# Rotated queries and keys of two chunks in one tile, for the first batch of a linear-attention and MoE kernel

## The chip, the cores and the metric

One core of a Trainium2 chip runs the whole program. The metric is the device time of one execution in microseconds (us). The engines are PE (matrix products), DVE (VectorE), ACT (ScalarE), POOL (GpSimd) and SP (the queue from which most transfers are issued).

## The reference, cut to what matters

Attention is a recurrence with a complex decay for every key feature; two MoE-like layers follow, the second behind a Fourier transform.

```python
# q, k, v, a_re, a_im: 4 batches, 8 heads, 768 steps, 48 features
scale = min(|a|, 0.999) / (|a| + 1e-6);  a = a * scale
for t in range(768):
    S_re, S_im = a.re*S_re - a.im*S_im + outer(k[t], v[t]),  a.re*S_im + a.im*S_re
    y[t] = q[t] @ S_re
u  = y + (U, V mixing of y over the steps)
x1 = u + relu(u @ w_ch1) @ w_ch2
u  = x1 + real(fft2(x1));  un = layernorm(u)
out = u + relu(un @ w_ch1') @ w_ch2'
```

## The kernel before

The recurrence is done in 6 chunks of 128 steps for each batch. Within a chunk the decay is split into a magnitude (folded into q and k) and an angle; q and k, multiplied by the cosine and sine of the summed angle, stand in 96 rows per head (48 features, real and imaginary). A chunk then needs the products of keys and queries (scores), a mask, the product with v, and a state that is carried to the next chunk. Chunks come in pairs m of two; `PAIRS` holds three pairs for each batch, and a tile that is loaded or made elementwise covers both chunks of a pair (index j).

`decays(m)` makes the magnitudes, `turns(m)` the angles. For the first pair (m = 0) `parts(m)` lets `turns` treat the two chunks one after the other, for all others at once. At its end `turns` writes for each chunk the tile QK: two copies of the end magnitudes (L426, the last two of 258 columns) and keys and queries times cosine and sine (L430, two VectorE instructions a chunk, for 2 x 3 rows of 128 steps each). Partition 8x + h of QK holds feature x of 16 and head h. The 96-row layout QT, in which features stand in partitions, is made by six transfers (L437): for each of z (cosine, sine) and i (three groups of 16 features) the 128 partitions of QK go to 16 partitions of QT, eight heads side by side, 258 floats (1032 bytes) from each partition. ScalarE makes the scaled keys from QK (L433).

`products(m, j)` consumes a chunk: scores on PE from QT (L462), masking on VectorE (`pm`, L467), transposed keys `kp` (L476) split into `k` (L481, L482), the state factor `fe` on POOL from QT (L537), the outputs `y` and the state sum `g` (L490), the state S (L564 on POOL, L575 on VectorE, L573 on ScalarE for the first).

`first_attention` runs batch 0 with nothing beside it but the first weights. Weights of the MoE layer come in 24 halves: a load into `stw` (L117, with buffers shared with `k` of batch 0, five in all), ACT L110, DVE L110, L132 and L133, a rounding copy on ACT (L147), and the low part on POOL (L148). `decays(3)`, for batch 1, is also written there. Then the MoE of batch 0 runs on PE (`hp` and `acc`, L93 to L95), with the attention of batch 1 beside it, and so on. A list scheduler sets the order on each engine from the program's priorities; at run time each engine runs its list in order, and an instruction that waits holds those behind it. At most eight transfers of the SP queue are under way: the ninth waits for the first.

Pools: `att` lives through all attention. `early` opens ahead of batch 0's attention and closes with it; `halves` opens then, in the memory that `early` leaves. Before the change QK and QT have two buffers in `att`, and chunks 2 and 5 of batch 0 have one in `early`:

```python
where = dict(pl=early[0], bufs=1) if b == 0 and c % 3 == 2 else dict(bufs=2)
QK = at(f"QK{b}_{c}", "QK", shape=(128, 2, 3, 258), **where)
QT = at(f"QT{b}_{c}", "QT", shape=(96, 8, 258), **where)
```

So chunk 3 takes chunk 0's buffers, chunk 4 chunk 1's, and chunk 5 chunk 2's.

Of the kernel before, what the change touches and what calls it, by code (L numbers as in the profile page):

```python
# [43 lines left out]
def mixer_kernel(ctx, tc, a_in, qk_in, v_in, u_in, v4_in, w_in, cc_in, ss_in, cb_in, sb_in, id_in, mask_in, rows_in, out):  # L44
    nc = tc.nc
# [13 lines left out]
    def bank(name, pool=None):  # L59
        pool = pool or pms  # L60
        return pool.tile([128, 512], F32, tag={id(pms): "ms", id(pacc): "acc", id(phid): "hid"}[id(pool)], name=name)
# [21 lines left out]
    def use(name):  # L83
        if table[0] != name:
            ordered(lambda: A.preload_act_table_set(name))
            table[0] = name

    def tabled(*args, **kw):
        ordered(lambda: A.activation(*args, **kw))  # L89
# [8 lines left out]
    early = [None]  # L98
# [121 lines left out]
    def attention_pool():  # L220
        pl = attp[0]

        def at(nm, tag=None, bufs=4, shape=(128, 3, 2, 128), dt=F32, pl=pl):
            return pl.tile(list(shape), dt, tag=tag or "t", name=nm, bufs=bufs)

        return at
# [32 lines left out]
    def row(x, i, js):  # L259
        return x[:, i, js].rearrange("p j t -> p (j t)")  # L260

    def flat(x):
        return x.rearrange("p i j t -> p (i j t)")

    def parts(m):

        return [slice(0, 1), slice(1, 2)] if m == 0 else [slice(0, 2)]
# [111 lines left out]
    def turns(m):  # L379

        b, cc = PAIRS[m]
        at = attention_pool()
        T_, Th, qf, kf, ends, turn, scaled = ew[m]
        use(TRIG)
        jj = parts(m)
        for js in jj:
            tabled(T_[:, :, js], T_[:, :, js], AF.Arctan, scale=1.0 / RE_MID)
        yield
        QKs = {}
        for js in jj:  # L390
            cy = carry.get(b)
            t, th = T_[:, :, js], Th[:, :, js]
            if len(jj) == 1:
                if cy is not None:
                    V.tensor_tensor(T_[:, :, 0, 0], T_[:, :, 0, 0], cy[:, :3], ALU.add)
                V.tensor_tensor_scan(out=flat(Th), data0=going, data1=flat(T_), initial=0.0, op0=ALU.mult, op1=ALU.add)
            else:
                for i in range(3):
                    V.tensor_tensor_scan(
                        out=row(Th, i, js),  # L400
                        data0=one.to_broadcast([128, 128]),
                        data1=row(T_, i, js),
                        initial=0.0 if cy is None else cy[:, i : i + 1],
                        op0=ALU.mult,
                        op1=ALU.add,
                    )
            if b == 0:
                V.tensor_scalar(t, th, 1.0 / (2 * PI), MAGIC, ALU.mult, ALU.add)
            else:
                A.activation(t, th, AF.Copy, bias=MAGIC, scale=1.0 / (2 * PI))  # L410
            V.scalar_tensor_tensor(out=th, in0=t.bitcast(I16)[:, :, :, 0::2], scalar=-2 * PI, in1=th, op0=ALU.mult, op1=ALU.add)
            c = cc[js.stop - 1]
            if c != NC - 1:
                carry[b] = at(f"cy{b}_{c}", "cy", 2, (128, 4))
                V.tensor_copy(carry[b][:, :3], Th[:, :, js.stop - 1, 127])
            tabled(t, th, AF.Sin, scale=1.0 - 2.0**-22)
            A.activation(th, th, AF.Abs)
            tabled(th, th, AF.Sin, bias=halfpi, scale=-1.0)
            yield
            if len(jj) == 1:  # L420
                yield
            for j in range(js.start, js.stop):
                c = cc[j]
                where = dict(pl=early[0], bufs=1) if b == 0 and c % 3 == 2 else dict(bufs=2)
                QK = at(f"QK{b}_{c}", "QK", shape=(128, 2, 3, 258), **where)
                V.tensor_copy(QK[:, :, :, 256:258], ends[:, :, j : j + 1].unsqueeze(1).to_broadcast([128, 2, 3, 2]))  # L426
                QT = at(f"QT{b}_{c}", "QT", shape=(96, 8, 258), **where)
                w = turn[:, :, :, j]
                for to, x in ((slice(128, 256), kf), (slice(0, 128), qf)):
                    V.tensor_tensor(QK[:, :, :, to], x[:, :, j].unsqueeze(1).to_broadcast([128, 2, 3, 128]), w, ALU.mult)  # L430
                if c != NC - 1:
                    for i in range(3):
                        A.activation(scaled[:, :, i, j], QK[:, :, i, 128:256], AF.Copy, scale=ends[:, i, j : j + 1])  # L433
                for z in range(2):
                    for i in range(3):
                        p0 = z * 48 + i * 16
                        nc.sync.dma_start(QT[p0 : p0 + 16], QK[:, z, i, :])  # L437
                qkt[b, c] = QT, scaled[:, :, :, j]
                yield

    def products(m, j):

        b, cc = PAIRS[m]
        c = cc[j]
        n = f"{b}_{c}"
        last = c == NC - 1
        plain = b <= 1
        at = attention_pool()

        def t3(nm, bufs, shape, dt=F32):  # L450
            return at(f"{nm}{n}", nm, bufs, shape, dt, attp[1] if dt == F16 else attp[0])

        QT, scaled = qkt[b, c]
        vin = inp["v", b, c]
        sc, pm, kp = [], [], []
        pool = pacc if b == 0 else pms

        def scores(hf):
            ps = bank(f"sc{n}_{hf}").rearrange("p (h t) -> p h t", h=4)
            for h in range(4):  # L460
                q = QT[:, hf * 4 + h]
                T.matmul(ps[:, h, :], q[:, 128:256], q[:, :128], start=True, stop=True)  # L462
            sc.append(ps)

        def masked(hf):
            pm.append(room[:, hf] if b == 0 else at(f"pm{n}_{hf}", "pm", 2, (128, 4, 128)))
            V.tensor_tensor(pm[hf], sc[hf], mask.unsqueeze(1).to_broadcast([128, 4, 128]), ALU.mult)  # L467
            if not plain:
                hs = slice(hf * 4, hf * 4 + 4)
                A.copy(ph[:, hs], pm[hf])  # L470
                V.tensor_tensor(plo[:, hs], pm[hf], ph[:, hs], ALU.subtract)
# [27 lines left out]
        if b == 0:  # L499
            if len(rooms) < 4:  # L500
                rooms.append(wpl.tile([128, 3, 4, 128], F32, tag="w", name=f"pm{n}"))
            room = rooms[c % 4]
# [12 lines left out]
        yield  # L515
        scores(1)
        masked(0)
        if not plain and c > 0:
            qh, ql = t3("qh", 1, (96, 8, 128), F16), t3("ql", 1, (96, 8, 128), F16)
            A.copy(qh, QT[:, :, :128])  # L520
            V.tensor_tensor(ql, QT[:, :, :128], qh, ALU.subtract)
        yield
        masked(1)
        if not last:
            if b == 0:
# [166 lines left out]
    def elementwise(m):  # L692
        return padded(chain(decays(m), turns(m)), 16) if m < len(PAIRS) else iter(())
# [4 lines left out]
    def attention(b):  # L698
        m = 3 * b
        yield from padded(urgent(turns(m), -300) if b == 1 else turns(m), 9)  # L700
        ahead = chain(elementwise(m + 1), elementwise(m + 2), decays(m + 3) if b + 1 < B else ())
        yield from zipped(chain(padded(both(m), 16 + LAG), padded(both(m + 1), 16), both(m + 2)), ahead)
# [5 lines left out]

    def first_attention(w1):
        run(zipped(decays(0), late(1, decays(1)), late(2, decays(2))), turns(0))  # L710
        with tc.high_priority(-800):
            load_uv()
# [233 lines left out]
    attp = [apool.enter_context(tc.tile_pool(name="att", bufs=2)), None]  # L946
# [20 lines left out]
    warm, wide = bank("warm", phid)[:, :256], ident  # L967
# [261 lines left out]
```

## Time and profile before

| | us |
|---|---|
| median of three runs (lowest, highest) | 1006.13 (1005.81, 1008.61) |
| the profiled execution, its own time | 1010.51 |
| span of the profiled execution | 1008.7 |
| PE busy in the span | 867.8 (86%) |
| DVE busy | 643.1 (64%) |
| ACT busy | 466.6 (46%) |
| POOL busy | 224.9 (22%) |
| share of the chain that ended last that is DMA QT<-QK | 8% |

The span runs from the first to the last instruction of one execution; the time of an execution holds it and what lies around it. Busy shares are means over stages with different limits, so a stage has to be read from its own windows. The chain that ended last is followed back from the last instruction, at each step to what released it. Idle time in a timeline row stands in square brackets, with what ended it; an engine that is not the bound of its stage loses nothing by it.

### The profile page before, as it was taken

The numbers are of one execution on the slowest core, as the hardware profiler recorded it, in microseconds if no ns is written. First come the engines' busy times: TensorE is split into PE (matmuls) and PEld (weight loads), VectorE is DVE, ScalarE is ACT, GpSimd is POOL, SyncE is SP. The second block draws the span as 40 slices with busy tenths as digits, with TensorE's granted clock in tenths as the row PEclk, the third lists the DMA queues.
The fourth block names the chain that finished last, engine by engine and source line by source line (L and its number), as shares of the span: only waits on it lengthen the run. The fifth ranks groups of instructions, "written<-read, shape, count | busy, mean of one in ns | idle before, by whom it ended". The sixth has DMA issues, their size and how long they took to land.

```text
span 1008.7 us, 16225 instructions
## 1 busy us (share of the span) xinstructions
PE 867.8 (86%) x6350; PEld 821.9 (81%) x6350; DVE 643.1 (64%) x1110; ACT 466.6 (46%) x891; POOL 224.9 (22%) x227
## 2 busy tenths in 40 slices
PE   0056858798898898989999999799999999999997
PEld 0045747787887898878999999689999999999997
DVE  7967696767567796787873539986535635453121
ACT  8556557565775877768742223453112212211111
POOL 4312362302012010120205216532401312010000
PEclk9998677988998999989999999999999999999999
DMA  9049546463653627346055114341210101000000
GB/s 355 1 64 155 146 136 131 102 102 104 103 95 79 104 79 119 81 91 105 9 88 204 40 32 134 109 149 33 65 46 17 58 23 47 1 25 24 1 24 27
DMA packets 47093, 83.39 MB, mean 83 GB/s; under 512 B 5600, under 2 KB 36064, under 8 KB 47008
## 3 DMA queue, kind: packets, MB, share of 16 engines
q1 hardware_dynamic: 45152, 75.96, 33.3%
q0 software_dynamic: 1856, 6.31, 1.9%
q8 instruction: 52, 0.85, 0.4%
q14 instruction: 33, 0.27, 0.1%
HBM read 53.79 MB, written 9.44 MB: 63 GB/s over the span
## 4 chain that ended last, share of the span: by engine, by line
PE 46%; DVE 24%; DMA 13%; ACT 8%; issue 4%; SPq 4%; POOL 1%; another core or an unknown queue 0%; ACTq 0%; DVEq 0%; POOLq 0%
DMA QT<-QK 8%; PE acc L95 6%; PE hp L93 6%; PE hp L95 6%; PE hp L94 6%; PE acc L93 6%; PE acc L94 6%; DMA stw<-in_w_dram 5%; SPq L437 4%; PE sc L462 3%; DVE ls L354 2%; DVE QK L430 2%; DVE wxw L133 1%; ACT ls L89 1%; DVE wxw L132 1%
## 5 line engine op out<-in xcount | busy, mean ns | idle before, releaser
L193 DVE SCALAR_TENSOR_TENSOR hl<-hp,hh 128x384 fp32r<-128x384 f32 x192 | 105.6, 552 | 201.0 <-ACT hh L191 193.3
L191 ACT ACTIVATE hh<-hp 128x384 fp32r<-128x384 f32 x192 | 93.4, 488 | 273.9 <-PE hp L95 253.7
L93 PE MATMUL acc<-w,hh 128*128 128x384 f32 x576 | 204.0, 354 | 5.9 <-ACT hh L191 4.8
L94 PE MATMUL acc<-w,hh 128*128 128x384 f32 x576 | 198.8, 345 | 0.0
L95 PE MATMUL acc<-w,hl 128*128 128x384 f32 x576 | 164.7, 351 | 17.6 <-DVE hl L193 17.4
L95 PEld LDWEIGHTS acc<-w,hl 128*128 128x128 f32 x576 | 106.4, 194 | 23.6 <-DVE hl L193 23.1
L93 PEld LDWEIGHTS acc<-w,hh 128*128 128x128 f32 x576 | 111.8, 194 | 10.5 <-ACT hh L191 8.6
L94 PEld LDWEIGHTS acc<-w,hh 128*128 128x128 f32 x576 | 112.3, 195 | 0.2
L93 PE MATMUL hp<-u,w 128*128 128x384 f32 x288 | 101.2, 355 | 11.4 <-ACT u L639 11.4
L94 PE MATMUL hp<-u,w 128*128 128x384 f32 x288 | 103.2, 358 | 0.0
L95 PE MATMUL hp<-u,w 128*128 128x384 f32 x288 | 101.8, 353 | 0.0
L94 PE MATMUL hp<-n,w 128*128 128x384 f32 x288 | 96.5, 335 | 1.4 <-DVE n L917 1.2
L95 PE MATMUL hp<-n,w 128*128 128x384 f32 x288 | 96.5, 335 | 0.0
L93 PE MATMUL hp<-n,w 128*128 128x384 f32 x288 | 96.3, 335 | 0.0
L462 PE MATMUL sc<-QT 96*128 96x128 f32 x384 | 59.8, 311 | 28.7 <-DMA QT<-QK 23.5
L462 PEld LDWEIGHTS sc<-QT 96*128 96x128 f32 x384 | 55.1, 219 | 32.9 <-issue 30.3
L148 POOL TENSOR_TENSOR w<-wxw,w 128x384 fp32r<-128x384 f32 x48 | 57.5, 1202 | 75.1 <-ACT w L147 72.9
L93 PEld LDWEIGHTS hp<-u,w 128*128 128x128 f32 x288 | 57.7, 202 | 12.8 <-ACT u L639 12.8
L94 PEld LDWEIGHTS hp<-u,w 128*128 128x128 f32 x288 | 57.5, 200 | 1.1 <-DVE u L640 0.8
L95 PEld LDWEIGHTS hp<-u,w 128*128 128x128 f32 x288 | 57.3, 199 | 0.4
L94 PEld LDWEIGHTS hp<-n,w 128*128 128x128 f32 x288 | 54.1, 188 | 2.0 <-DVE n L917 2.0
L537 POOL TENSOR_SCALAR fe<-QT 96x8 f32<-96x8 f32 x20 | 6.5, 325 | 216.4 <-DMA QT<-QK 211.4
(285 smaller groups left out, 1747.3 us busy)
## 6 DMA issues: line engine op xcount, KB each, us to landing
QT<-QK SPq DMA_DIRECT2D x144, 129.0 KB
stw<-in_w_dram SPq DMA_DIRECT2D x48, 384.0 KB
ain<-in_a_dram SPq DMA_DIRECT2D x12, 768.0 KB
qkin<-in_qk_dram SPq DMA_DIRECT2D x12, 768.0 KB
x1d<-x SPq DMA_DIRECT2D x24, 192.0 KB
vin<-in_v_dram SPq DMA_DIRECT2D x18, 192.0 KB
lo<-x1d SPq DMA_DIRECT2D x12, 192.0 KB
out_dram<-lo SPq DMA_DIRECT2D x12, 192.0 KB
```

The lines of the kernel that those rows point to most:

```text
L89: ordered(lambda: A.activation(*args, **kw))
L93: T.matmul(o, ah, bh, start=start, stop=False, skip_group_check=skip)
L94: T.matmul(o, ah, bl, start=False, stop=False, skip_group_check=skip)
L95: T.matmul(o, al, bh, start=False, stop=stop, skip_group_check=skip)
L132: V.scalar_tensor_tensor(out=xi, in0=xi, scalar=3, in1=low, op0=ALU.logical_shift_left, op1=ALU.bitwise_or)
L148: G.tensor_tensor(w[:, 1, zs], x, f32(w[:, 0, zs]), ALU.subtract)
L191: A.activation(hh, hp, AF.Relu)
L193: V.scalar_tensor_tensor(out=hl, in0=hp, scalar=0.0, in1=f32(hh), op0=ALU.max, op1=ALU.subtract)
L354: V.tensor_tensor_scan(out=flat(s1), data0=starts, data1=flat(s1), initial=1.0, op0=ALU.max, op1=ALU.mult)
L430: V.tensor_tensor(QK[:, :, :, to], x[:, :, j].unsqueeze(1).to_broadcast([128, 2, 3, 128]), w, ALU.mult)
L437: nc.sync.dma_start(QT[p0 : p0 + 16], QK[:, z, i, :])
L462: T.matmul(ps[:, h, :], q[:, 128:256], q[:, :128], start=True, stop=True)
```

## The change

For batch 0 one tile QK holds both chunks of a pair, with the two chunks side by side for each z and i, and one tile QT likewise. It has one buffer for QK and two for QT, both in `early`. For the first pair the six transfers are still issued for each chunk (1032 bytes from each partition); for the second and third pair they are issued once, when the second chunk's products are done, and carry both chunks (2064 bytes from each partition). For the other batches a tile holds one chunk as before, in two buffers, but in `halves`. The masked scores `pm` of the later batches move to `halves` as well.

```diff
@@ turns
-        QKs = {}
+        wide = b == 0
+        n_j = 2 if wide else 1
+        pl = early[0] if b == 0 else attp[1]
         for js in jj:
...
             for j in range(js.start, js.stop):
                 c = cc[j]
-                where = dict(pl=early[0], bufs=1) if b == 0 and c % 3 == 2 else dict(bufs=2)
-                QK = at(f"QK{b}_{c}", "QK", shape=(128, 2, 3, 258), **where)
+                if j == 0 or not wide:
+                    QKs = at(f"QK{b}_{c}", "QK", 1 if wide else 2, (128, 2, 3, n_j, 258), pl=pl)
+                    QTs = at(f"QT{b}_{c}", "QT", 2 if b == 0 or not wide else 1, (96, 8, n_j, 258), pl=pl)
+                jw = j if wide else 0
+                QK, QT = QKs[:, :, :, jw], QTs[:, :, jw]
                 V.tensor_copy(QK[:, :, :, 256:258], ends[:, :, j : j + 1].unsqueeze(1).to_broadcast([128, 2, 3, 2]))
-                QT = at(f"QT{b}_{c}", "QT", shape=(96, 8, 258), **where)
                 w = turn[:, :, :, j]
                 for to, x in ((slice(128, 256), kf), (slice(0, 128), qf)):
                     V.tensor_tensor(QK[:, :, :, to], x[:, :, j].unsqueeze(1).to_broadcast([128, 2, 3, 128]), w, ALU.mult)
+                if not wide or m == 0 or j == 1:
+                    at_j = slice(jw, jw + 1) if m == 0 else slice(0, n_j)
+                    for z in range(2):
+                        for i in range(3):
+                            p0 = z * 48 + i * 16
+                            nc.sync.dma_start(
+                                QTs[p0 : p0 + 16, :, at_j].rearrange("p h j t -> p h (j t)"),
+                                QKs[:, z, i, at_j].rearrange("p j t -> p (j t)"),
+                            )
                 if c != NC - 1:
...
-                for z in range(2):
-                    for i in range(3):
-                        p0 = z * 48 + i * 16
-                        nc.sync.dma_start(QT[p0 : p0 + 16], QK[:, z, i, :])
                 qkt[b, c] = QT, scaled[:, :, :, j]
@@ products, masked
-            pm.append(room[:, hf] if b == 0 else at(f"pm{n}_{hf}", "pm", 2, (128, 4, 128)))
+            pm.append(room[:, hf] if b == 0 else at(f"pm{n}_{hf}", "pm", 2, (128, 4, 128), pl=attp[1]))
```

The scheduler makes a new order of it on all engines, up to about 300 us of the profile; behind that the order is the same on each. In the names below the first digit is the batch and the next the chunk (or, for `stw` and `w`, the layer, f and half); the last number only tells buffers apart.

SP's queue, from the transfers of chunk 0 on, before:

```order
L437 DMA QT0_0_225<-QK0_0_223 16x8x258 x6
L437 DMA QT0_1_249<-QK0_1_247 16x8x258 x6
L437 DMA QT0_2_331<-QK0_2_329 16x8x258 x6
L437 DMA QT0_3_354<-QK0_3_352 16x8x258 x6
L117 DMA stw0_0_0_594<-in_w_dram 128x768
L117 DMA stw0_0_1_596<-in_w_dram 128x768
L117 DMA stw0_1_0_606<-in_w_dram 128x768
L437 DMA QT0_4_415<-QK0_4_413 16x8x258 x6
L437 DMA QT0_5_457<-QK0_5_455 16x8x258 x6
L117 DMA stw0_1_1_711<-in_w_dram 128x768
```

and now:

```order
L440 DMA QT0_0_224<-QK0_0_223 16x8x258 x12
L117 DMA stw0_0_0_576<-in_w_dram 128x768
L440 DMA QT0_2_328<-QK0_2_327 16x8x516 x6
L117 DMA stw0_0_1_578<-in_w_dram 128x768
L117 DMA stw0_1_0_588<-in_w_dram 128x768
L440 DMA QT0_4_404<-QK0_4_403 16x8x516 x6
L117 DMA stw0_1_1_693<-in_w_dram 128x768
```

The first weight load stands ahead of chunk 2's transfers; the transfers of chunks 2 and 3, and of 4 and 5, are six with rows of twice the length.

VectorE (DVE) around the rotation of chunks 4 and 5, before:

```order
L408 TENSOR_SCALAR ain0_4_116<-ain0_4_116 128x768
L426 COPY QK0_5_455<-fe0_4_165 128x6x2
L411 SCALAR_TENSOR_TENSOR ain0_4_116<-ain0_4_116 128x768
L467 TENSOR_TENSOR pm0_2_493<-sc0_2_0_494,mask_82 128x512
L467 TENSOR_TENSOR pm0_2_493<-sc0_2_1_505,mask_82 128x512
L575 SCALAR_TENSOR_TENSOR S0_1_565<-g0_1_564,S0_1_565 96x384
L430 TENSOR_TENSOR QK0_4_413<-qkin0_4_122,ain0_4_116 128x6x128 x2
L430 TENSOR_TENSOR QK0_5_455<-qkin0_4_122,ain0_4_116 128x6x128 x2
```

and now:

```order
L410 TENSOR_SCALAR ain0_4_116<-ain0_4_116 128x768
L413 SCALAR_TENSOR_TENSOR ain0_4_116<-ain0_4_116 128x768
L431 COPY QK0_4_403<-fe0_4_165 128x6x2 x2
L434 TENSOR_TENSOR QK0_4_403<-qkin0_4_122,ain0_4_116 128x6x128 x4
L110 TENSOR_SCALAR stw0_0_0_576<-stw0_0_0_576 128x384
L476 TENSOR_TENSOR pm0_2_475<-sc0_2_0_476,mask_82 128x512
```

Both copies of a pair now stand right before its rotation, and the rotation of chunks 4 and 5 stands before the masking of chunk 2, where it stood behind it. In the same way the copy for chunk 3 no longer stands ahead of chunk 1's rotation.

VectorE around the masking of chunk 4, before:

```order
L341 SCALAR_TENSOR_TENSOR ls1_0_470<-ls1_0_470 128x768
L467 TENSOR_TENSOR pm0_0_288<-sc0_4_0_732,mask_82 128x512
L467 TENSOR_TENSOR pm0_0_288<-sc0_4_1_740,mask_82 128x512
L354 SCALAR_TENSOR_TENSOR ls1_0_470<-starts_103,ls1_0_470 128x768
L482 SCALAR_TENSOR_TENSOR k0_4_747<-kp0_4_0_748,k0_4_747 128x8x48
L482 SCALAR_TENSOR_TENSOR k0_4_747<-kp0_4_1_754,k0_4_747 128x8x48
L132 SCALAR_TENSOR_TENSOR wxw0_1_0_714<-wxw0_1_0_714,stw0_1_0_606 128x384
L110 TENSOR_SCALAR stw0_1_1_711<-stw0_1_1_711 128x384
```

and now:

```order
L476 TENSOR_TENSOR pm0_3_599<-sc0_3_1_608,mask_82 128x512
L110 TENSOR_SCALAR stw0_1_1_693<-stw0_1_1_693 128x384
L521 SCALAR_TENSOR_TENSOR v0_3_605<-vin0_0_126,v0_3_605 128x384
L132 SCALAR_TENSOR_TENSOR wxw0_1_0_696<-wxw0_1_0_696,stw0_1_0_588 128x384
L133 SCALAR_TENSOR_TENSOR wxw0_1_0_696<-stw0_1_0_588,wxw0_1_0_696 128x384
L110 TENSOR_SCALAR stw0_2_0_703<-stw0_2_0_703 128x384
L584 SCALAR_TENSOR_TENSOR S0_2_664<-g0_2_663,S0_2_664 96x384
L328 SCALAR_TENSOR_TENSOR ls1_2_1316<-ls1_2_1316 128x768
L363 SCALAR_TENSOR_TENSOR turn1_0_451<-ls1_0_452,turn1_0_451 128x768
L476 TENSOR_TENSOR pm0_0_286<-sc0_4_0_714,mask_82 128x512
```

The first instruction on the weight half stw0_1_1 stood behind the masking of chunk 4 and stands ahead of it now, with part of batch 1's decays.

## Rows read from the trace of the kernel before

**Rows 1.** The page's head: span and instructions.
```profile
span 1008.7 us, 16225 instructions
```

**Rows 2.** Busy time by window: stretch, length, then PE, PEld, DVE, ACT, POOL.
```profile
core 0: us, PE busy (x) PEld busy (x) DVE busy (x) ACT busy (x) POOL busy (x), PEclk, DMA share, GB/s
48.00:112.00 64.00, 39.59 (x458) 34.30 (x459) 43.21 (x69) 32.71 (x65) 16.14 (x13) 0.85 0.75 118
...
92.00:112.00 20.00, 12.86 (x182) 11.80 (x182) 13.04 (x23) 8.66 (x19) 6.96 (x7) 0.69 0.94 161
112.00:160.00 48.00, 34.58 (x296) 28.28 (x294) 40.48 (x66) 29.04 (x58) 22.98 (x16) 0.77 0.43 125
160.00:300.00 140.00, 121.58 (x993) 111.05 (x994) 96.98 (x139) 92.21 (x171) 26.40 (x19) 0.89 0.55 106
300.00:520.00 220.00, 199.78 (x1693) 189.10 (x1692) 170.75 (x257) 155.33 (x285) 27.68 (x20) 0.95 0.48 87
520.00:1008.70 488.70, 472.27 (x2916) 459.14 (x2914) 249.93 (x532) 123.52 (x260) 112.22 (x136) 0.99 0.18 55
```

**Rows 3.** Timeline of the SP queue, 44 to 130 us: start, length, instruction, count.
```profile
53.37 29.09 SPq L437 DMA_DIRECT2D QT<-QK  x24
```

**Rows 4.** The chain that ended last, 44 to 131 us: start, length, what.
```profile
56.67 5.35 DMA QT<-QK
...
77.28 5.19 DMA QT<-QK
...
97.70 5.38 DMA QT<-QK
```

**Rows 5.** Transfers in the window 78 to 88 us.
```profile
DMA packets 1310, 1.20 MB, mean 120 GB/s; under 512 B 145, under 2 KB 1310, under 8 KB 1310
...
q1 hardware_dynamic: 1310, 1.20, 114.9%
```

**Rows 6.** Transfers in the window 54 to 62 us; GB/s in 40 slices of 0.2 us.
```profile
GB/s 0 0 0 77 186 263 134 139 237 232 129 160 139 124 103 124 160 114 98 103 124 160 119 114 114 98 145 134 124 103 93 72 41 0 0 0 0 0 0 0
DMA packets 864, 0.79 MB, mean 99 GB/s; under 512 B 96, under 2 KB 864, under 8 KB 864
```

**Rows 7.** Timeline of DVE, 48 to 135 us; in brackets idle before, and its end.
```profile
57.19 1.02 DVE L482 SCALAR_TENSOR_TENSOR k<-kp,k 128x384 f16<-128x384 f32 x2 [1.27 <-ACT k L481]
62.14 0.17 DVE L426 COPY QK<-fe 128x12 f32<-128x12 f32 x1 [3.93 <-DMA QT<-QK]
...
64.24 0.69 DVE L467 TENSOR_TENSOR pm<-sc,mask 128x512 f32<-128x512 f32 x1
...
72.77 0.17 DVE L426 COPY QK<-fe 128x12 f32<-128x12 f32 x1 [2.92 <-DMA QT<-QK]
72.87 3.57 DVE L430 TENSOR_TENSOR QK<-qkin,ain 128x768 f32<-128x768 f32 x4
...
80.20 0.55 DVE L408 TENSOR_SCALAR ain<-ain 128x768 f32<-128x768 f32 x1
83.71 0.17 DVE L426 COPY QK<-fe 128x12 f32<-128x12 f32 x1 [2.96 <-issue]
83.79 0.97 DVE L411 SCALAR_TENSOR_TENSOR ain<-ain 128x768 f32<-128x768 int16 x1
...
105.31 0.69 DVE L467 TENSOR_TENSOR pm<-sc,mask 128x512 f32<-128x512 f32 x1 [3.23 <-PE sc L462]
```

**Rows 8.** Timeline of ACT, 48 to 135 us.
```profile
58.89 0.61 ACT L89 ACTIVATE ain<-ain,halfpi 128x384 f32<-128x384 f32 x1
...
71.78 0.93 ACT L89 ACTIVATE ain<-ain,halfpi 128x768 f32<-128x768 f32 x1
```

**Rows 9.** Transfers in the window 2 to 20 us, the first loads.
```profile
DMA packets 2155, 7.15 MB, mean 397 GB/s; under 512 B 304, under 2 KB 1200, under 8 KB 2155
...
q1 hardware_dynamic: 2155, 7.15, 101.7%
```

**Rows 10.** Timeline of PE, 130 to 215 us: the first MoE matmuls.
```profile
139.55 1.01 PE L93 MATMUL hp<-u,w 128*128 128x384 f32 x2 [4.82 <-ACT u L639]
```

## The prediction

> **What bounds the kernel now.** I read the page's span, then the windows by stage, then the chain of waits and the timelines of single engines between 44 and 140 us, where the change sits. The profiled execution has a span of 1008.7 us [rows 1] and took 1010.5 us as a whole; the median of the three runs is 1006.1. Everything below is worked out inside the span and laid on that median.
>
> The windows [rows 2] show two kernels in one. From 520 us on PE is busy 472 of 489 us, from 300 to 520 us 200 of 220: there PE is the bound. Before 160 us it is not: from 48 to 112 us VectorE works 43.2 of 64 us and from 112 to 160 us 40.5 of 48, PE less than either. The written order of all engines, compared instruction by instruction, is the same in both kernels from about 300 us on, so whatever the change gives or costs is made before that, and reaches the end as a shift. The in-order engine with the most work in the stretch is VectorE: it makes the rotated tiles, masks the scores, and converts the weights that the MoE needs next. I therefore count its idle time: 20.8 us from 48 to 112 us, 7.5 us from 112 to 160 us [rows 2].
>
> **What a transpose costs.** Six transfers carry one chunk. The first of chunk 0 is issued at 53.37 us [rows 3] and the last lands at 56.67 + 5.35 = 62.02 us [rows 4]: 8.65 us alone. When two chunks queue, the window 78 to 88 us moves 120 GB/s [rows 5], so a further 0.79 MB (the bytes of six, [rows 6]) takes 6.6 us: a pair takes 15.2 us from its first issue to its last landing. Within the pair of chunks 2 and 3 the first one lands early, at 77.28 + 5.19 = 82.5 us [rows 4].
>
> **The change, part by part.**
>
> *Chunks 0 and 1.* They keep their 1 KB packets and six transfers each. What goes is the copy into QK of chunk 3 in front of chunk 1's rotation, for which VectorE waits 3.93 us until chunk 0 has landed [rows 7]. The rotation then waits only for ScalarE's cosine, done at 58.89 + 0.61 = 59.5 us [rows 8]: 1.3 us of idle instead of 3.9. It ends at 61.3 us, and chunk 1's transfers are issued some 2.7 us earlier. Late next is the masking of chunk 0, which cannot start before 64.24 us [rows 7], since its scores wait for the same landing as before: 2.8 us of new idle. Chunk 2's rotation started at 72.87 us behind a 2.92 us wait for chunk 1's landing [rows 7]; that landing now comes near 70, but the cosine ends at 71.78 + 0.93 = 72.7 us [rows 8]. Same idle, 2.9 us. So the earlier landing of chunk 1 buys nothing.
>
> *Chunks 2 and 3.* Six transfers of twice the size replace twelve. The six issues saved (0.6 us each on the sync queue) cost nothing now: data moves slower than issues come. The first is issued when both rotations are done, 72.8 + 3.57 = 76.35 us [rows 7], half of the four rotations (1.8 us) later than now. The price of a 2 KB packet between two SBUF tiles stands in no row. Lower bound: it takes no longer than a 1 KB one, then the pair lands after 8.65 us. Upper bound: bytes decide, 15.2 us. I take the upper one. In the crowded window the 1310 packets took 114.9% of 16 engines for 10 us, 140 ns each [rows 5], but the first transfers of chunk 0, alone, ran at 186 to 263 GB/s and fell to 100 to 125 GB/s only when several stood in line [rows 6]. A fixed price per packet would show from the first packet on; a shared limit on bytes into the 16 destination partitions would not. So both chunks land at 76.35 + 15.2 = 91.6 us: chunk 2 nine microseconds later than now, chunk 3 about two.
>
> [...]
>
> *The single QK buffer.* Chunk 4's copy, and behind it VectorE, now waits for that landing. The eight instructions before it end at about 81.7 us (80.20 + 0.55, plus 0.97 for the int16 step that stands behind the copy now, [rows 7]). Wait: 91.6 − 81.7 = 9.9 us, in place of 2.96 us at chunk 5's copy [rows 7]. Rotating chunks 4 and 5 takes 3.57 + 0.2 us: issue at 95.4, landing of both at 110.6 us, against 97.70 + 5.38 = 103.1 us for chunk 4 now [rows 4].
>
> *The weight loads.* One moves ahead of chunk 2's transfers, two stay behind them, and the fourth (stw0_1_1) stands behind chunk 4's. Its 0.39 MB take 1.0 us at 397 GB/s [rows 9], so it lands at 111.6 us. VectorE's shift of it is now in front of chunk 4's masking instead of behind it. The 16 instructions ahead take 16 × 0.567 us (13.04 us for 23, [rows 2]) = 9.1 us and end at 104.5: a wait of 7.1 us, where VectorE now waits 3.23 us for chunk 4's scores [rows 7].
>
> *The pools.* Masked scores, QK and QT of the later batches open in the memory of the early pool. Their first writers wait for the last read of batch 0's QT, which comes just before the end of batch 0's attention; the first one that matters, QK of batch 1, is rotated some 25 us later. Nothing, covered by the weight conversions.
>
> **The sum.** Idle of VectorE up to 111.6 us: 1.3 (unchanged, [rows 7]) + 1.3 + 2.8 + 2.9 + 9.9 + 7.1 + 0.4 for the state = 25.7 us, against 20.8: 4.9 us later. Behind that the same work follows. From 160 to 300 us PE has 18 us idle [rows 2] that can take some of it, and more weights are converted before the MoE begins, so its first matmul need not wait 4.82 us for u [rows 10]. I cannot order these two exactly; between nothing carried (1006) and all carried (1011), I take half: +2.4 us, **1008.5 us**.
>
> About 0.3%, or 3 us, is what a measurement of this kernel can tell from no change.
>
> **Rivals.**
>
> *Packets set the price.* For it: a load packet of 3.3 KB on average takes 136 ns (2155 packets in 101.7% of 16 engines for 18 us, [rows 9]), no less than a queued 1 KB one. Then a pair lands after 8.65 us: 85.0 and 97.4 us; VectorE waits 3.3 instead of 9.9 and 0.5 instead of 7.1. Idle 12.5 us, 8 less than now; with a wait for chunk 4's scores again and the weights as next limit, −5 us: 1001 us. Against it: the fast start in [rows 6]. [...] Chance 0.19.
>
> *The tail of batch 0's attention moves as a block (slower).* Chunk 4's scores start at 110.6 instead of 103.1 us, and the weights cannot use the gap, since the next load stands in the same line behind the transfers. If the path from chunk 4's scores to the first MoE matmul (139.55 us, [rows 10]) keeps its 36 us, everything shifts by 7.5 us: 1013.6 us. It decides if that matmul starts after 145 us. Chance 0.21.
>
> *The new order pays.* The waits behind 112 us shrink by more than the 4.9 us: the 4.82 us at u and some of the 7.5 us go, because weights up to f = 5 are ready first. Net −1 to −5 us, 1003 us. It decides if the first MoE matmul comes before 139 us. Chance 0.14.
>
> *The packets are not joined.* If the access pattern still breaks at 1 KB, bytes and waits are as in my forecast, with the same end. Chance 0.02.
>
> **How the numbers follow.** My forecast has 0.44, with 1004 to 1012 as its own range. Faster by over 0.3%: the packet rival 0.19 and 0.08 of the order rival = 0.27. Slower: 0.21 and 0.14 of the forecast (the upper part of its range) = 0.35. Same: 0.30 + 0.06 + 0.02 = 0.38. The range of 999 to 1014 takes in both outer rivals' prices and leaves their far ends out.
>
> **What would show it.** Right: transfers of chunks 2 and 3 still moving about 120 GB/s for 13 us; a VectorE wait of 8 to 11 us at chunk 4's QK copy near 82 us; a second of 5 to 8 us at a weight shift near 105 us; chunk 4's scores near 110 us. Wrong: a pair that lands within 10 us of its first issue, or no second wait; or, with both waits there, a first MoE matmul outside 138 to 145 us.

## The result, and the profile after

| | us |
|---|---|
| before, median of 20 executions | 1005.93 |
| with the change, median | 1011.34 |
| ratio, 95% interval | 1.0058 (1.0043 to 1.0072) |
| profiled execution with the change, its own time and span | 1009.56, 1007.8 |

The change costs 5.4 us (by the interval 4.3 to 7.2). That is inside the range of 999 to 1014 and over the forecast of 1008.5. One of the 20 executions with the change took 1684 us; the ratio leaves it out.

The ends of the two profiled executions can't be set against each other: the one of the kernel before took 1010.5 us, 4.6 above its median, the one of the change 1.8 below its own. A second trace of each (runs e7, e8) and one of a kernel with the same order as before (e2) help: the table gives all five, for the places that the prediction named and for three behind them.

| start, us | before | e7 | e2 | change | e8 | shift of the means |
|---|---|---|---|---|---|---|
| scores of chunk 4 | 103.22 | 102.91 | 104.24 | 112.20 | 112.19 | +8.7 |
| first MoE matmul (`hp`) | 139.55 | 134.68 | 137.13 | 147.91 | 148.47 | +11.1 |
| first accumulating product (`acc`) | 150.59 | 145.72 | 148.18 | 154.04 | 153.88 | +5.8 |
| masking of batch 1's chunk 3 | 235.21 | 233.65 | 235.80 | 241.34 | 241.56 | +6.6 |
| masking of batch 1's chunk 4 | 270.39 | 267.50 | 269.70 | 269.14 | 269.36 | +0.1 |
| end of the span | 1008.7 | 1008.6 | 1005.8 | 1007.8 | 1009.3 | +0.9 |
| idle of VectorE, 48 to 113 us (its length) | 21.3 | 19.6 | 21.4 | 25.3 | 25.7 | +4.7 |

First the windows of the changed kernel, as in [rows 2]: stretch, length, busy time of PE, PEld, DVE, ACT, POOL.

```profile
core 0: us, PE busy (x) PEld busy (x) DVE busy (x) ACT busy (x) POOL busy (x), PEclk, DMA share, GB/s
48.00:112.00 64.00, 29.96 (x344) 25.55 (x344) 39.56 (x61) 30.34 (x57) 13.75 (x10) 0.86 0.72 100
112.00:160.00 48.00, 40.09 (x391) 33.93 (x392) 41.31 (x70) 28.17 (x60) 22.01 (x18) 0.78 0.44 141
160.00:300.00 140.00, 123.61 (x1004) 112.75 (x1003) 97.26 (x142) 95.18 (x175) 28.02 (x20) 0.88 0.56 110
```

Up to 112 us, PE does 9.6 us less and VectorE 3.7 us less than in [rows 2]; from 112 to 300 us PE catches up on 7.5 of it, VectorE on 1.1. The sync queue and VectorE show where it goes:

```profile
76.45 3.86 SPq L440 DMA_DIRECT2D QT<-QK  x6
...
96.25 3.84 SPq L440 DMA_DIRECT2D QT<-QK  x6
```

```profile
81.34 0.96 DVE L413 SCALAR_TENSOR_TENSOR ain<-ain 128x768 f32<-128x768 int16 x1
92.38 0.27 DVE L431 COPY QK<-fe 128x12 f32<-128x12 f32 x2 [10.08 <-DMA QT<-QK]
...
112.85 0.72 DVE L110 TENSOR_SCALAR stw<-stw 128x384 int32<-128x384 int32 x1 [6.74 <-DMA stw<-in_w_dram]
...
118.83 0.68 DVE L476 TENSOR_TENSOR pm<-sc,mask 128x512 f32<-128x512 f32 x1
```

The six issues of the pair are over in 3.9 us, yet it lands at 92.3, 15.9 us behind its first issue. VectorE waits 10.08 us for it, then 6.74 us for a weight half that stands behind the next pair. In [rows 7] the same two places held 2.96 and 3.23 us. The transfers of the first pair in the window 76 to 93 us (GB/s in 40 slices of 0.425 us; then the issues, their size and median time to landing):

```profile
GB/s 0 0 0 29 180 233 214 102 102 131 151 83 121 112 97 155 117 97 102 126 151 97 112 112 97 136 151 83 107 126 97 146 124 114 116 116 188 383 376 434
...
QT<-QK SPq DMA_DIRECT2D x6, 258.0 KB, 8.6
```

Packets of 2064 bytes start at 180 to 233 GB/s and fall to 117 GB/s (the mean of the 29 slices after that), much as those of 1032 bytes do in [rows 6]. The weights behind them then run at 376 GB/s and more.

On PE the tail begins later, and the waits for u have gone. Before, the first MoE product starts at 139.55 us behind a wait for u [rows 10], the second group waits for u again, and the accumulating product comes 11.04 us after the first one:

```profile
144.99 1.01 PE L93 MATMUL hp<-u,w 128*128 128x384 f32 x2 [2.97 <-ACT u L639]
...
150.59 0.69 PE L93 MATMUL acc<-w,hh 128*128 128x384 f32 x1 [1.09 <-ACT hh L191]
```

and with the change, where it comes 6.13 us after:

```profile
112.20 3.75 PE L471 MATMUL sc<-QT 96*128 96x128 f32 x16 [10.02 <-DMA QT<-QK]
...
147.91 0.42 PE L93 MATMUL hp<-u,w 128*128 128x384 f32 x1
...
154.04 0.44 PE L93 MATMUL acc<-w,hh 128*128 128x384 f32 x1 [2.27 <-ACT hh L191]
```

The vanished waits are the smaller part of this gain. The same stretch as windows, before and with the change (the third number from the end is the clock granted to PE, as a share of full speed):

```profile
139.55:150.59 11.04, 6.98 (x19) 5.21 (x19) 10.62 (x15) 7.84 (x16) 5.73 (x6) 0.50 0.27 72
```

```profile
147.91:154.04 6.13, 3.87 (x21) 2.96 (x18) 5.43 (x10) 4.34 (x9) 1.01 (x1) 1.00 0.04 6
```

PE worked 6.98 us at a granted clock of 0.50 before and 3.87 us at 1.00 with the change: 3.1 of the 4.9 us. Its idle time in the stretch fell by 1.8 us. Before, PE had just waited 4.82 us for u; with the change it came to its first MoE product without a wait.

In the traced executions the delay is then made up. Batch 1's attention stays 6.6 us late up to its chunk 3, and at its chunk 4 nothing of it is left (the table). Between the two, from 233 to 250 us, PE has idle time before and little with the change:

```profile
233.00:250.00 17.00, 12.38 (x135) 10.56 (x134) 14.29 (x22) 9.29 (x18) 3.14 (x1) 0.89 0.21 67
```

```profile
233.00:250.00 17.00, 16.07 (x226) 14.10 (x225) 13.48 (x23) 12.07 (x23) 5.47 (x3) 1.00 0.21 72
```

The longest wait of PE in it, before:

```profile
247.16 1.33 PE L95 MATMUL acc<-w,hl 128*128 128x384 f32 x3 [2.52 <-DVE hl L193]
```

PE is idle for 4.6 us before (3.8 and 4.8 in e7 and e2) and for 0.9 us with the change (0.6 in e8); the granted clock was 0.89 before and 1.00 with the change. Yet the medians differ by 5.4 us, where the ends of these traces differ by 0.9. The three traced executions of the old order took 1.1 to 4.6 us more than the medians of their runs, the two of the change 0.3 and 1.8 us less, so they do not show where a typical execution loses the 5.4 us.

So the experiments had two questions: which part of the change costs, and what the limit on the transfers is.

### The profile page after: what moved, and what is told of

Its sections match the earlier page's. It is cut to its first block, busy times and chain, and to the rows that moved or that the text cites. A ratio compares the mean times of both kernels' runs of the same rounds, so it can differ in the third digit from the quotient of the medians.

```text
span 1007.8 us, 16190 instructions
## 1 busy us (share of the span) xinstructions
PE 863.1 (86%) x6350; PEld 817.1 (81%) x6350; DVE 640.6 (64%) x1110; ACT 465.4 (46%) x891; POOL 223.6 (22%) x227
## 4 chain that ended last, share of the span: by engine, by line
PE 48%; DVE 23%; DMA 12%; ACT 8%; issue 4%; SPq 3%; POOL 1%; DVEq 0%; ACTq 0%; POOLq 0%
DMA QT<-QK 7%; PE acc L95 7%; PE acc L93 7%; PE hp L95 6%; PE hp L94 6%; PE hp L93 6%; PE acc L94 6%; DMA stw<-in_w_dram 4%; SPq L440 3%; PE sc L471 2%; DVE ls L354 2%; ACT ls L89 1%; DVE wxw L133 1%; DVE hl L193 1%; DVE wxw L132 1%
## 5 line engine op out<-in xcount | busy, mean ns | idle before, releaser
L93 PE MATMUL acc<-w,hh 128*128 128x384 f32 x576 | 201.6, 350 | 4.7 <-ACT hh L191 3.8
L94 PE MATMUL acc<-w,hh 128*128 128x384 f32 x576 | 195.9, 340 | 0.0
L93 PEld LDWEIGHTS acc<-w,hh 128*128 128x128 f32 x576 | 109.7, 190 | 9.4 <-ACT hh L191 6.8
L94 PEld LDWEIGHTS acc<-w,hh 128*128 128x128 f32 x576 | 109.9, 191 | 0.2
L93 PE MATMUL hp<-u,w 128*128 128x384 f32 x288 | 99.6, 349 | 2.6 <-ACT u L648 2.6
L94 PE MATMUL hp<-u,w 128*128 128x384 f32 x288 | 101.0, 351 | 0.0
L95 PE MATMUL hp<-u,w 128*128 128x384 f32 x288 | 100.2, 348 | 0.0
L471 PE MATMUL sc<-QT 96*128 96x128 f32 x384 | 62.9, 321 | 42.1 <-DMA QT<-QK 36.1
L471 PEld LDWEIGHTS sc<-QT 96*128 96x128 f32 x384 | 58.0, 228 | 46.3 <-issue 44.2
L93 PEld LDWEIGHTS hp<-u,w 128*128 128x128 f32 x288 | 56.2, 196 | 3.5 <-ACT u L648 3.4
L94 PEld LDWEIGHTS hp<-u,w 128*128 128x128 f32 x288 | 56.2, 195 | 0.6 <-DVE u L649 0.3
L95 PEld LDWEIGHTS hp<-u,w 128*128 128x128 f32 x288 | 56.0, 195 | 0.4
```

The lines of the kernel that those rows point to most:

```text
L93: T.matmul(o, ah, bh, start=start, stop=False, skip_group_check=skip)
L94: T.matmul(o, ah, bl, start=False, stop=False, skip_group_check=skip)
L95: T.matmul(o, al, bh, start=False, stop=stop, skip_group_check=skip)
```

## Experiments

**Joining undone (e1).** Wide tiles, single QK buffer and pools stay, but each chunk is sent on its own. The order on all engines then is nearly that of before.

```diff
-                if not wide or m == 0 or j == 1:
-                    at_j = slice(jw, jw + 1) if m == 0 else slice(0, n_j)
+                if True:
+                    at_j = slice(jw, jw + 1)
```

> The changed kernel with the joining undone: every chunk of batch 0 is sent by six transfers of its own (1032 bytes a packet) behind its own rotation; the wide tiles, the single QK buffer and the pools stay. Main theory (the joined transfer is what costs: it holds chunk 2 back until both chunks have landed): chunk 2's scores start near 84 us again (92.4 with the change, 83.7 before), VectorE's wait ahead of QK4's copy is 1 to 4 us instead of 10.1, since chunk 3 lands near 91 us and the masking of chunk 2 comes first, and the time is 1006 to 1008 us. Rival 'single buffer': the wait for the landing of both chunks makes most of the loss by itself; then the time stays at 1010 to 1012 us.

Measured: 1007.59 us, ratio to before 1.0013 (0.9993 to 1.0033). Scores of chunk 2 on PE, and the copy for chunk 4 on VectorE:

```profile
82.52 3.39 PE L471 MATMUL sc<-QT 96*128 96x128 f32 x16 [2.89 <-issue]
```

```profile
88.72 0.28 DVE L431 COPY QK<-fe 128x12 f32<-128x12 f32 x2 [1.32 <-DMA QT<-QK]
```

The twelve transfers of chunks 2 and 3 in that kernel, window 72 to 92 us (slices of 0.5 us):

```profile
GB/s 0 0 0 0 0 116 184 215 147 107 134 105 136 109 130 109 120 118 112 136 103 138 103 132 114 130 107 118 126 126 156 104 276 393 399 414 381 221 12 18
```

From the first byte at 74.5 us to VectorE's release at 88.7 they take 14.2 us in packets of 1032 bytes; with the change the same bytes take 15.0 us (77.3 to 92.3) in packets of 2064. The longer packets were no faster. Chunk 2 is back at 82.5 us and the wait for the buffer is 1.3 us instead of 10. With 1.0058 for the whole change, the joining (with the order that the scheduler makes of it; the two were not separated) is worth 0.45%, some 4.5 of the 5.4 us. Chunk 4's scores start at 99.98 us there, 3.5 us earlier than in the order of before, and the time is no better for it: the start of chunk 4 alone does not set the end. What is left for the single buffer can't be told from nothing.

**The pools alone (e2).** The kernel before with QK and QT of batch 0 in three buffers each in `early`, the others and `pm` in the later pool.

```diff
-                where = dict(pl=early[0], bufs=1) if b == 0 and c % 3 == 2 else dict(bufs=2)
+                where = dict(pl=early[0], bufs=3) if b == 0 else dict(bufs=2, pl=attp[1])
...
-            pm.append(room[:, hf] if b == 0 else at(f"pm{n}_{hf}", "pm", 2, (128, 4, 128)))
+            pm.append(room[:, hf] if b == 0 else at(f"pm{n}_{hf}", "pm", 2, (128, 4, 128), pl=attp[1]))
```

> The kernel before, with the memory placement alone changed: QK and QT of batch 0 in three buffers each in the early pool, those of the other batches and their masked scores in the later pool. The order on every engine is that of before. Main theory: nothing waits for that memory, 1005 to 1007 us, the ratio to before includes 1. Rival 'placement': later batches wait for batch 0's tiles to be read, or land in worse memory, and it costs 2 us or more.

Measured: 1006.51 us, 1.0008 (0.9991 to 1.0024). The pools cost nothing that can be measured, as predicted.

**Other destination rows, batch 0 alone (e3 on the kernel before, e4 on the change).** The same 16 features of a transfer go to every second one of 32 rows.

```diff
-                        p0 = z * 48 + i * 16
-                        nc.sync.dma_start(QT[p0 : p0 + 16], QK[:, z, i, :])
+                        to = slice(i * 32 + z, i * 32 + 32, 2) if b == 0 else slice(z * 48 + i * 16, z * 48 + i * 16 + 16)
+                        nc.sync.dma_start(QT[to], QK[:, z, i, :])
...
+            if b == 0:
+                dh, dl = (k.rearrange("t (h x z) -> t h x z", h=8, z=2)[:, :, :, z] for k in (kh, kl))
+            else:
+                dh, dl = (k.rearrange("t (h z x) -> t h z x", h=8, z=2)[:, :, z, :] for k in (kh, kl))
```

> The kernel before, batch 0 alone: the 16 features of a transfer go to every second one of 32 partitions of QT (row 2x+z) instead of 16 neighbouring ones, and the transposed keys are split into the same order of rows. Bytes, packets, transfers and orders stay. Main theory (bytes into the destination partitions limit a transfer): queued transfers move 160 to 220 GB/s instead of about 120; chunk 0's six are down within 7.3 us of the first issue instead of 8.65; a pair becomes limited by the issues on the queue (12 at 0.64 us and some 2 us to the last landing, 9.7 us instead of 15.2); VectorE's 20.8 us of idle from 48 to 112 us shrink by 4 to 9 us, and the time is 997 to 1002 us. Rival 'packets or the queue are the limit': the rate stays at 120 GB/s and the time at 1006. [...]

> The changed kernel with the same spread of the destination rows. Main theory: the pair of chunks 2 and 3 lands 8 to 11 us behind its first issue instead of 15.9, so the wait ahead of QK4's copy falls from 10.1 to 3 to 6 us, the second wait at the weight shift to 0 to 3 us, and the time is 998 to 1004 us; with fewer issues it is no slower than the spread kernel with single chunks by more than 3 us. Rival 'packets or the queue are the limit': the pair still takes 15 to 16 us and the time stays near 1011. Rival 'order': the transfers get faster, but the time stays above 1008, since the order of the other engines is what costs.

Measured: e3 991.22 us, 0.9852 (0.9832 to 0.9871); e4 997.00 us, 0.9905 (0.9886 to 0.9923). The transfers of chunk 0 in e3, window 54 to 62 us, to be read against [rows 6]:

```profile
GB/s 0 0 0 0 119 191 279 114 160 268 207 181 243 196 160 227 238 150 186 268 160 196 258 155 10 0 0 0 0 0 0 0 0 0 0 0 0 0 0 0
DMA packets 864, 0.79 MB, mean 99 GB/s; under 512 B 96, under 2 KB 864, under 8 KB 864
```

Same bytes, same packets, but they are down by 59.0 us instead of 60.6, and no slice sags to 100. Chunk 4's scores start at 91.6 us instead of 103.2. In e4 the pair of chunks 2 and 3 (window 73 to 86 us) and VectorE's wait for it:

```profile
GB/s 0 0 0 0 0 76 197 197 375 343 222 191 203 210 260 210 210 235 222 210 229 191 191 203 197 248 216 253 208 265 397 397 397 406 192 0 0 0 0 0
...
QT<-QK SPq DMA_DIRECT2D x6, 258.0 KB, 4.8
```

```profile
83.31 0.27 DVE L431 COPY QK<-fe 128x12 f32<-128x12 f32 x2 [4.41 <-DMA QT<-QK]
```

The rate is about 215 GB/s, the pair lands 9.7 us behind its first issue (73.62 us) and the wait is 4.41 us. So what held the transfers at 117 GB/s is the neighbourhood of the destination rows, neither packets nor the queue: with the same packets of 2064 bytes, in six transfers on the same queue, every second one of 32 rows takes about 215. Both times came out better than expected, e3 by 6 us and e4 by 1 us beyond their ranges; e4 was to be at most 3 us slower than e3 and is 5.8. The second wait has gone in e4 (0.48 us at that weight shift), but chunk 4's scores start at 96.95 instead of 91.55 us. Joining loses its lead time at either rate.

**The second wait, two attempts (e5, e9).** e5 issues the load of stw0_1_1 from ScalarE's queue:

```diff
-        nc.sync.dma_start(st.rearrange("p n w -> p (n w)"), src.bitcast(I32))
+        (A if name == "w0_1_1" else nc.sync).dma_start(st.rearrange("p n w -> p (n w)"), src.bitcast(I32))
```

> The changed kernel, with the load of the weight half stw0_1_1 issued from ScalarE's queue instead of the sync queue, where it stands behind the transfers of chunks 4 and 5. Main theory (the landing of chunk 4 sets the path, and the second wait only lies beside it): the load lands ahead of that pair, the 6.74 us wait at its shift goes, and VectorE waits 4 us or more for chunk 4's scores instead, which start near 112 us as before; the time stays at 1008.5 to 1012 us. Rival 'the second wait is a cost of its own' (a term of 7.1 us in the prediction's sum): the time falls by some 5 us, to 1005 to 1007.

Measured: 1011.97 us, 1.0069 (1.0049 to 1.0089). The issue, and the load's way:

```profile
99.79 0.38 ACTq L117 DMA_DIRECT2D stw<-in_w_dram  x1
```

```profile
stw<-in_w_dram ACTq DMA_DIRECT2D x1, 384.0 KB, 11.9
```

ScalarE issued it 0.9 us behind the last issue of the pair (95.11 + 3.81 = 98.92 us), so it was not ahead of the pair as meant. It took 11.9 us on a queue of its own, and the wait stayed at 5.37 us: the experiment did not take away what it meant to. From 99 to 108 us only the sync queue (q1) moves packets; those of ScalarE's (q10) all come from 108 to 112 us:

```profile
q1 hardware_dynamic: 571, 1.05, 108.3%
```

```profile
q1 hardware_dynamic: 147, 0.61, 55.5%
q10 hardware_dynamic: 144, 0.39, 49.2%
```

So a queue of its own brought nothing here: its packets did not mix with the pair's before 108 us, 3 us ahead of chunk 4's scores (111.05 us). e9 moves the work instead: what waits for loads behind the pair goes behind chunk 4's masking.

```diff
+                if c == 3:
+                    anchor()
-                for _ in range((0, 2, 2, 2, 2, 2)[c]):
+                for _ in range((0, 2, 1, 3, 2, 2)[c]):
...
-                    A.activation(s2_, im, AF.Square, scale=0.5)
+                    (kept if m == 4 else lambda f, *a, **k: f(*a, **k))(A.activation, s2_, im, AF.Square, scale=0.5)
```

> The changed kernel, with the work that waits for loads behind the transfers of chunks 4 and 5 put behind chunk 4's masking: the first steps on the weight half stw0_1_1 and the first squares of batch 1's second pair. Main theory (the landing of chunk 4 is what is late): no wait of over 3 us ahead of chunk 4's masking other than for its scores; the masking starts near 114.5 us instead of 118.8, yet the first MoE product comes within 3 us of 148 as now, and the time is 1009 to 1012 us. Rival 'the second wait is a cost of its own' (term of 7.1 us): the first MoE product comes 4 us or more earlier, and the time falls to 1004 to 1007.5.

Measured: 1013.00 us, 1 us over the range, 1.0062 (1.0038 to 1.0085); first MoE matmul at 148.24 us. The masking came at 119.36, not 114.5: another wait stood in the place of the one removed, against the expectation of none over 3 us. On VectorE, POOL and ScalarE:

```profile
113.85 0.56 DVE L132 SCALAR_TENSOR_TENSOR wxw<-wxw,stw 128x384 int32<-128x384 int32 x1 [6.48 <-ACT wxw L110]
```

```profile
112.08 0.20 POOL L546 TENSOR_SCALAR fe<-QT 96x8 f32<-96x8 f32 x1 [5.86 <-DMA QT<-QK]
112.25 0.99 POOL L148 TENSOR_TENSOR w<-wxw,w 128x384 fp32r<-128x384 f32 x1
```

```profile
113.27 0.55 ACT L110 ACTIVATE wxw<-stw 128x384 f32<-128x384 f32 x1 [5.75 <-POOL w L148]
```

POOL, in its written order, waits for chunk 4's column of QT ahead of the low part of weight half w0_0_1; that low part frees the buffer that ScalarE's step on the next half fills, for which VectorE waits. So VectorE, ScalarE and POOL stand at the same landing, and taking one wait away there gains nothing. Whether the second wait costs time of its own stays open, since neither run brought the masking forward to 114.5 us.

**Other destination rows in all batches (e6 on the kernel before, e10 on the change), and every sixth row (e11).**

```diff
-                        p0 = z * 48 + i * 16
-                        nc.sync.dma_start(QT[p0 : p0 + 16], QK[:, z, i, :])
+                        p0 = i * 32 + z
+                        nc.sync.dma_start(QT[p0 : p0 + 31 : 2], QK[:, z, i, :])
```

In e11 the rows are `QT[i * 2 + z : i * 2 + z + 91 : 6]`, and the transposed keys are written in that order, `kp[z].rearrange("t (x i h) -> t i x h", i=3, h=8)[:, i]`.

> The kernel before with the destination rows spread in all batches, not only in the first; the order of the engines in the later batches changes with it. Main theory: behind the first batch the transposes lie beside matrix products that set the pace, so nothing more is to be had: 989 to 994 us, where the spread of the first batch alone gave 991.2. Rival 'the later batches wait for transposes too': below 988.

> The changed kernel with the destination rows spread (every second of 32) in all batches. Main theory (joining holds the first chunk of a pair back, at any rate of the transfers, and saves nothing that is late): slower than the same spread with single chunks (963.1 us) by 3 to 7 us: 966 to 970. Rival 'with fast transfers the issues are the price, and joining halves them': 958 to 963.

> The kernel before, with the features in every sixth of the 96 rows in all batches (row 6x'+2i+z; the transposed keys are written in the same order), so that a transfer covers the whole height of the tile. Main theory (the neighbourhood of the destination rows sets the rate): queued transfers reach 215 GB/s or more, now limited by an issue each 0.64 us (129 KB in 0.64 us are 206 GB/s); the time within 4 us of that with every second row, 959 to 967. Rival 'every second row was special': back to about 120 GB/s and 1000 us or more.

Measured: e6 963.12 us, 0.9598 (0.9565 to 0.9631); e11 965.59 us, 0.9599 (0.9576 to 0.9623); e10 978.33 us, 0.9716 (0.9694 to 0.9739). e6 beats both kernels by 4 to 5%, and my theory missed it by some 26 us: I held the later transposes to be covered. They were not. Groups of the kernel before in the window 160 to 520 us (behind the second bar: idle time ahead of the group, and what ended it):

```profile
L462 PE MATMUL sc<-QT 96*128 96x128 f32 x272 | 38.2, 288 | 12.0 <-DMA QT<-QK 9.7 <-issue 1.2 <-ACT y L583 1.1
L520 ACT CAST qh<-QT 96x1024 f16<-96x1024 f32 x9 | 9.4, 1043 | 21.4 <-DMA QT<-QK 19.5 <-issue 1.8
```

and of e6:

```profile
L462 PE MATMUL sc<-QT 96*128 96x128 f32 x288 | 41.2, 290 | 6.9 <-DVE u L640 3.2 <-DMA QT<-QK 2.5 <-DVE S L575 1.1
...
L520 ACT CAST qh<-QT 96x1024 f16<-96x1024 f32 x10 | 10.4, 1042 | 6.6 <-DMA QT<-QK 3.3 <-PE y L490 3.0 <-issue 0.2
```

PE waited 9.7 us and ScalarE 19.5 us for transposes, 2.5 and 3.3 in e6. The scheduler also gave e6 another order in the later batches; how much of the 28 us beyond e3 is that was not separated. Every sixth row brings no more than every second: around the transfers of chunks 2 and 3, e6 moves 182 GB/s from 71.5 to 79 us and e11 194 from 72 to 79.5. Six issues take 3.80 us (e4), some 0.64 us each; 129 KB in that time are 206 GB/s. So that the queue's issues are the limit in both is an estimate, worked out from these numbers. e10 stands 12 us (by the ratios) above e6, more than expected; chunk 4 starts at 96.98 there and at 89.34 in e6, which may account for 7.6. The rest may be the order of the engines in the later batches, which differs too, or the tiles' other places there; that stays open.

**Second traces (e7, e8).** No edit.

> The kernel before once more, for a second trace of it, since the first was of an execution above its median. Main theory (from the landing of chunk 4 the path to the first MoE product takes 36 us in every kernel): chunk 4's scores start between 99 and 104 us, the first MoE matmul 35.5 to 37 us later.

> The changed kernel once more, for a second trace of it. Main theory: the wait ahead of QK4's copy is 9 to 11 us again, chunk 4's scores start between 110.5 and 113 us, and the first MoE matmul 35 to 37.5 us later; so the shift there is 7 to 11 us against the kernel before, of which 4 to 7 us are left at the end once the granted clock is alike. Rival: the distance from chunk 4's scores to the first MoE matmul differs by over 3 us from that of the kernel before, and the end follows something else.

Measured: 1006.00 and 1011.41 us; e8 stands to the kernel before at 1.0060 (1.0036 to 1.0084). Chunk 4's scores came where both were expected. The first MoE matmul did not in e7: it came 31.8 us later, not 35.5 to 37. This stretch has 36.3 us in the first trace of the kernel before and 32.9 in e2, against 35.7 and 36.3 with the change. What tells them apart is the granted clock, not the kernel. The first trace of before, e7 and the change:

```profile
103.22:139.55 36.33, 28.02 (x346) 24.08 (x346) 27.21 (x46) 16.50 (x37) 17.17 (x12) 0.78 0.55 160
```

```profile
102.91:134.68 31.77, 24.96 (x346) 21.04 (x346) 26.56 (x46) 16.28 (x37) 17.98 (x12) 0.88 0.62 183
```

```profile
112.20:147.91 35.71, 30.80 (x355) 25.88 (x355) 30.09 (x52) 20.34 (x47) 18.45 (x15) 0.78 0.50 164
```

At 0.78 to 0.80 the stretch takes some 36 us in both kernels, at 0.86 and 0.88 (e2, e7) 32 to 33. So the second trace does not bear out the rival of a different distance: of the shift of 11.1 us at the first MoE matmul, 8.7 are chunk 4's and the rest goes with the clock.

## Why the prediction was right or wrong

*Transfers: right.* A pair was to take 15.2 us and took 15.9; the rate was to stay at 120 GB/s and was 117. The reason given, bytes into 16 neighbouring partitions, is shown by e3 and e4: about 215 GB/s with the rows spread in e4, and in e3 chunk 0's six down at 59.0 us instead of 60.6. The packet rival fell: the row that was to bear it out (85.0 us for chunk 2) reads 92.3.

*The two waits: right.* 9.9 us were forecast at the copy for chunk 4 and 10.08 and 9.69 measured; 7.1 at the weight shift, 6.74 and 6.72 measured. The sum said 25.7 us of idle against 20.8, the traces, to 113 us, 25.5 against 20.8.

*Pools, single buffer: right as far as it can be told.* The intervals of e2 and e1 include 1.

*The step that failed is the carry: "between nothing carried and all carried I take half: +2.4 us".* The median lost 5.4 us, all of the 4.9 forecast. The half stood on no row, and the traces do not show a half either. The delay is 8.7 us at chunk 4, 11.1 at the first MoE matmul, 5.8 at the first accumulating one, and 0.1 at chunk 4 of batch 1. The idle time of PE that was to take some of it did so in these executions: from 233 to 250 us it fell from 4.6 to 0.9 us. The waits for u went as forecast. Why the medians lose all of it even so, and where, stays open. That the loss comes so near to VectorE's extra idle time (4.9 forecast, 4.7 measured) is therefore not shown to be more than luck.

*The rival "tail moves as a block" had the mark* (first MoE matmul after 145 us: 147.91), *and its path kept 36 us where the granted clock was alike, but a price 2 us too high*: in the traces the block does not reach the end. The median lies between it and the forecast. The text itself named this case as wrong: both waits there, and a first MoE matmul outside 138 to 145 us.

## What to carry to other kernels

When a transfer between two tiles is slow, look at which partitions it writes before its packets are made longer: here the same bytes ran at 117 GB/s into 16 neighbouring rows and at 215 into every second one of 32, and a free choice of row order was worth 4%, with the order that the scheduler made of it. Joining two transfers makes the first consumer wait for the last byte: chunk 2's scores started at 92.44 us here, and at 82.52 with each chunk sent on its own (e1). It lost with 16 neighbouring rows, and also with the rows spread (e4 5.8 us slower than e3, e10 12 us, by the ratios, than e6). And a delay read at one place is not yet the loss of the kernel: here it was 8.7, 11.1, 5.8 and 0.1 us at four places of the same traces. It is to be followed to the end, in more than one trace, with the granted clock beside it and with the traced executions' own times held against the median.

## What the runs showed of the hardware

A load on a queue of its own did not pass transfers that stood at a slow destination: 0.39 MB, worth 1.0 us at the 397 GB/s of [rows 9], took 11.9 us on ScalarE's queue, issued 0.9 us behind the pair on the sync queue (e5). That slow transposes so delay other loads as well, and that this is a part of why their rate mattered far behind the first batch was not tried by itself. And joining transfers gave nothing between two tiles: 15.0 us from the first byte to the landing in six of 258 KB with packets of 2 KB, against 14.2 in twelve of half the size.
